# A SwiGLU down product in fp32: eight block products of 512 columns become seven of 256 columns

## The chip, the core and the metric

The kernel runs on one core of one Trainium2 chip. The metric is the device time of one execution in microseconds. Before the change it is 600.21 us (median of three runs, 599.43 to 602.72). A core has five engines with queues of their own: PE (TensorE, matmuls; its weight loads are shown apart as PEld), DVE (VectorE), ACT (ScalarE), POOL (GpSimd) and SP, which here issues all the DMAs. Matmuls read SBUF and write PSUM, of which the feed-forward part uses eight tiles of 512 fp32 columns by 128 partitions (called banks below). All of POOL's operations in this kernel are on SBUF.

## The reference, cut to what matters

```python
x = A_q                                   # 2048 tokens x 512
h = _layernorm(x) * (1 + ca) + sa
x = x + ga * _A_ref(h, ...)               # a long causal convolution: first 200 us of the kernel
h = _layernorm(x) * (1 + cb) + sb
g = _silu(h @ w_gate)                     # 512 x 1792
u = h @ w_up
x = x + gb * ((g * u) @ w_down)           # 1792 x 512
```

Everything is fp32. The change concerns the last three lines, the feed-forward network, for the second half of the tokens.

## The kernel before, in words

**Precision.** A matmul here takes operands in the format fp32r. Each operand x is kept as two tensors, a high part (x copied to fp32r by ACT) and a low part (x minus the high part, by DVE or POOL). A product is three passes: low by high, high by low, high by high (`PASSES`, line 633). `wd_hi` and `wd_lo` (lines 620, 624) do it for a piece of w_down, `finish` (line 707) for an activation.

**Tiling.** The 1792 hidden columns are 14 blocks f of 128; two blocks are a group g (G = 2, seven groups). The 2048 tokens are two halves q of 1024, each of them two tiles t of 512 (xt[0] to xt[3], in which the result is accumulated). The program writes out n = 2 to 27, with q = n // 14 and f = n % 14 (loop at line 1415): first all blocks of the first 1024 tokens, then all of the second.

**Gate and up.** For one block, `gate_up` (line 714) computes gate and up for both token tiles at once by a 2x2 block scheme of seven products in place of eight. `seventh` (line 637) is one of them: six matmuls of 512 columns into one PSUM bank. The products run in the order 1, 5, 7, 2, 3, 6, 4 in the banks a, b, c, a, b, d, c; DVE adds them up, ACT applies silu, DVE multiplies gate by up. The weights' operands (three blocks A and four sums S, high and low) are made by `split_w` (line 585): casts on ACT, sums and low parts on POOL. It is done anew for each token half.

**Down.** `down` (line 648) is one 128-token block i of one tile t: six matmuls of 512 columns (two blocks f, three passes) into one bank, then a DVE addition to xt. Eight such downs make a group, 48 matmuls. They are put between the products of the two blocks after the group's end (`downs`: one behind product 7, one behind product 3, two behind product 6). The last group's eight come at the very end, and each then stores its rows.

**Order.** Each engine runs its instructions in the order in which the program writes them (`keep_in_program_order`), and each waits only for its data and buffers. What is not part of a block's own chain is hung behind one of its products: `at[k]` is a list of calls made behind product k. In n, `split_w(n + 1)` and `load_w(n + 2)` hang behind product 7, and behind product 3 comes the split of w_down for a group (odd f) or its load (even f). Loads go through SP in program order.

Of the kernel before, what the change touches and what calls it, by code (L numbers as in the profile page):

```python
# [10 lines left out]
F32 = mybir.dt.float32  # L11
F32R = mybir.dt.float32r
AF = mybir.ActivationFunctionType
ALU = mybir.AluOpType
# [41 lines left out]
def adaln_h3_swiglu(ctx, tc, q, kT, vT, shk, ssm, dskip, wgu, wdn, c, wmod, e_fwd, e_inv, w_c, out):  # L56
# [12 lines left out]
    homes8 = iter(  # L69
        "401235670135260172635162432634623634642623634642652376243652376243"  # L70
    )

    def e8(shape, dt, name):
        return wp.tile(shape, dt, tag=f"e8_{next(homes8)}", name=name, bufs=1)

    def r4(shape, dt, name):
        return wp.tile(shape, dt, tag="r4", name=name, bufs=5)
# [31 lines left out]
    def one(name):  # L109
        return ffn["p"].tile([P, 512], F32, tag="one", name=name) if "p" in ffn else bank(name)  # L110
# [474 lines left out]
    def split_w(f):  # L585
# [11 lines left out]
        s = e8([P, 2, 4, 2, P], F32R, "wsum")  # L597
# [6 lines left out]
        o = AOP[f] = {n: w[:, :, i] for i, n in enumerate(("A11", "A12", "A22"))}  # L604
        o.update({n: s[:, :, i] for i, n in enumerate(("S1", "S2", "S3", "S4"))})

    def w8_hi(f):

# [11 lines left out]
    def wd_hi(g):  # L620
        wt = WD[g] = e8([P, 2, G, D], F32R, "wd")
# [6 lines left out]
    def split_wd(g):  # L628
        wd_mul(g)
        wd_hi(g)  # L630
        wd_lo(g)

    PASSES = ((1, 0), (0, 1), (0, 0))
    PROD = {1: ("A11", "B11"), 2: ("A12", "B21"), 3: ("S4", "B22"), 4: ("A22", "T4"),
# [32 lines left out]
    def downs(n):  # L667
        for _ in range(min(n, len(todo))):
            down(*todo.pop(0))

    GU, SG = {}, {}

# [34 lines left out]
    def finish():  # L707

        if late:
            h, c_ = late.pop()  # L710
            act.copy(h[:, 0], c_)
            dve.tensor_tensor(h[:, 1], c_, h[:, 0].bitcast(F32), op=ALU.subtract)

    def gate_up(q, f, at={}):


        def behind(n):
            for fn in at.get(n, ()):
                fn()

        a = one("a")
        seventh(a, f, 1)
        p1 = g2("p1")
        act.copy(p1, a)
        behind(1)
        b = one("b")
        seventh(b, f, 5)
        p5 = g2("p5")
        act.copy(p5, b)
        finish()  # L730
        behind(5)
        c_ = one("c")
        seventh(c_, f, 7)
        dve.tensor_tensor(p5, p5, c_, op=ALU.add)
        behind(7)
        downs(1)
        seventh(a, f, 2, True)
        sg1 = g2("sg1")
        act.activation(sg1, a, AF.Silu)
        behind(2)  # L740
        seventh(b, f, 3, True)
        behind(3)
        downs(1)
        d = one("d")
        seventh(d, f, 6)
        dve.tensor_tensor(p1, p1, d, op=ALU.add)
        sg2 = g2("sg2")
# [4 lines left out]
        downs(2)  # L752
        dve.tensor_tensor(d, sg2, d, op=ALU.mult)
        h2 = acts[q, f, 1] = slots.pop(0)
        act.copy(h2[:, 0], d)
        seventh(c_, f, 4, True)
        dve.tensor_tensor(h2[:, 1], d, h2[:, 0].bitcast(F32), op=ALU.subtract)
        dve.tensor_tensor(c_, p1, c_, op=ALU.add)
        dve.tensor_tensor(c_, sg1, c_, op=ALU.mult)
        h1 = acts[q, f, 0] = slots.pop(0)  # L760
        late.append((h1, c_))
        behind(4)


    csil = cp.tile([P, 4], F32, name="csil")
    csb = cp.tile([P, 4, 32], F32, name="csb")

    def load_shk():
        sp.dma_start(shk_sb, shk.rearrange("(b p) t -> p b t", p=P))
# [30 lines left out]
        t = SS[c_][0:1, 0, :]  # L800
        dve.tensor_tensor(t, t, dsk[:, c_ * P : (c_ + 1) * P], op=ALU.add)

    wc = cp.tile([P, 384], F32, name="wc")
    WX, WK = wc[:, 0:96], wc[:, 96:192]
    def load_wc():
        sp.dma_start(wc, w_c)
# [573 lines left out]
    def release(n):  # L1380
# [31 lines left out]
        (14, 7): lambda: diff("B21", "B21", "B11"),  # L1412
        (14, 2): lambda: then("T4", "B21"),
    }
    for n in range(G, 2 * NF):
        q, f = n // NF, n % NF

        at = {k: [AT[n, k]] if (n, k) in AT else [] for k in range(1, 8)}
        if n + 1 < 2 * NF:
            at[7].append(lambda nf=(n + 1) % NF: split_w(nf))  # L1420
            if n + 2 < 2 * NF:
                at[7].append(lambda nf=(n + 2) % NF: load_w(nf))
            if f % G == G - 1:
                at[3].append(lambda g=(n + 1) % NF // G: split_wd(g))
            elif n + 2 < 2 * NF:
                at[3].append(lambda g=((n + 2) % NF) // G: load_wd(g))
        gate_up(q, f, at)
        if f % G == G - 1:
            todo += [(q, f // G, t, i) for t in (1, 0) for i in range(4)]
    finish()  # L1430
    downs(8)

# [55 lines left out]
```

## Time and profile before

| | |
|---|---|
| median of three runs | 600.21 us (599.43 to 602.72) |
| profiled execution, span | 598.0 us (first to last instruction; the execution's own time outside the span is not in the profile) |
| instructions | 10148 |
| granted PE clock, mean | 0.992 |
| DVE, ACT, POOL busy | 457.0, 302.7, 329.9 us |
| DMA | 69.00 MB in all |
| second half of the tokens | from about 388 us on |

PE's busy time counts modelled ends of matmuls; the starts are measured, so how often one starts is a better measure of its cost. In the timeline, "x6" is a run of six instructions merged into one line, with the start of the first and the time until the end of the last, and a bracket tells how long the engine stood idle before it and who ended that. In the groups, the number after the bar is the busy time in us, then the mean of one in ns. In the table of stretches a line has the stretch, its length, then for PE, PEld, DVE, ACT and POOL the busy us with the number of instructions, the granted clock of PE, the DMA share and GB/s.

### The profile page before, as it was taken

Reading aid. Unit: us, or ns where it says so; the run is one execution under the profiler, and the core shown is the slowest. Engines: PE = TensorE matmul, PEld = TensorE weight load, DVE = VectorE, ACT = ScalarE, POOL = GpSimd, SP = SyncE. Lnnn points to the kernel's source line nnn. Section 1 sums busy time; section 2 is a strip of 40 time slices with the busy share of each in tenths; the row PEclk is TensorE's granted clock in tenths of the full one; section 3 lists DMA queues with packets and bytes.
Section 4 is the critical chain, followed back from the end, with each engine's and each line's share of the span. In section 5 each row is a group of like instructions: output and inputs, shape, how many; then the busy total and the mean of one; then the engine's idle time right before and its main releaser. Section 6 shows DMA issues by size and latency. Waiting matters only on the chain.

```text
span 598.0 us, 10148 instructions
## 1 busy us (share of the span) xinstructions
PE 583.2 (98%) x4132; PEld 455.0 (76%) x4132; DVE 457.0 (76%) x585; ACT 302.7 (51%) x443; POOL 329.9 (55%) x264
## 2 busy tenths in 40 slices
PE   5999999999999999999999999999999999999997
PEld 4955756535988888888888888788888888888875
DVE  6999989978968878787778868975656565656555
ACT  1897989953574454445544435443434343434320
POOL 0003269692395896757467765766747474747200
PEclk7999999999999999999999999999999999999999
DMA  8998999999011021212120201243212110210003
GB/s 289 412 392 308 227 340 299 210 332 172 33 41 65 21 92 35 71 36 71 36 71 35 71 36 36 71 144 103 71 36 70 36 70 37 70 36 0 1 1 140
DMA packets 35423, 69.00 MB, mean 115 GB/s; under 512 B 2481, under 2 KB 18993, under 8 KB 33074
## 3 DMA queue, kind: packets, MB, share of 16 engines
q1 hardware_dynamic: 35378, 68.37, 37.0%
q8 instruction: 32, 0.52, 0.4%
q14 instruction: 13, 0.11, 0.1%
HBM read 55.78 MB, written 12.58 MB: 114 GB/s over the span
## 4 chain that ended last, share of the span: by engine, by line
PE 85%; DMA 6%; ACT 3%; DVE 2%; SPq 2%; issue 2%; ACTq 0%; DVEq 0%
PE dn L40 25%; PE a L40 12%; PE b L40 11%; PE c L40 11%; PE d L40 6%; PE s L40 5%; PE g L40 3%; DMA X<-away 2%; PE iv L40 2%; PE y L40 2%; PE px L40 2%; PE pk L40 2%; SPq L40 2%; DMA away<-X 2%; PE kt L40 1%
## 5 line engine op out<-in xcount | busy, mean ns | idle before, releaser
L40 PE MATMUL dn<-wd,acts 128*128 128x512 f32 x672 | 166.4, 391 | 0.5 <-DVE acts L40 0.4
L40 PEld LDWEIGHTS dn<-wd,acts 128*128 128x128 f32 x672 | 125.7, 188 | 27.6 <-DVE acts L40 1.1
L40 POOL TENSOR_TENSOR wa<-ws,wa 128x512 fp32r<-128x512 f32 (+1 forms) x52 | 61.7, 1209 | 111.8 <-ACT wa L40 104.0
L40 DVE TENSOR_TENSOR x<-x,dn 128x512 f32<-128x512 f32 x112 | 74.9, 681 | 50.6 <-PE dn L40 49.4
L40 PE MATMUL b<-op,wsum 128*128 128x512 f32 x312 | 79.2, 389 | 0.0
L40 POOL TENSOR_TENSOR wsum<-sr,wsum 128x1024 fp32r<-128x1024 f32 x26 | 71.4, 2745 | 0.0
L40 PEld LDWEIGHTS b<-op,wsum 128*128 128x128 f32 x312 | 58.5, 188 | 12.2
L40 ACT ACTIVATE sg<-sg 128x512 f32<-128x512 f32 x26 | 16.5, 633 | 85.4 <-DVE sg L40 85.4
L40 PE MATMUL a<-op,wa 128*128 128x512 f32 x228 | 57.9, 389 | 0.0
L40 PEld LDWEIGHTS a<-op,wa 128*128 128x128 f32 x228 | 42.8, 188 | 8.9
L40 DVE STREAM_TRANSPOSE X<-X 128x1024 f32<-128x1024 f32 x20 | 46.2, 2338 | 1.1 <-ACT X L40 1.1
L40 ACT CAST acts<-d 128x512 fp32r<-128x512 f32 x26 | 15.3, 587 | 62.5 <-DVE d L40 38.1
L40 POOL TENSOR_TENSOR vt<-u,vt 128x512 f32<-128x512 f32 x8 | 10.1, 1303 | 64.9 <-DMA x<-in_q 50.8
L40 POOL TENSOR_TENSOR s<-s,bcs 128x1024 f32<-128x1024 f32 x16 | 38.8, 2449 | 9.5 <-ACT s L40 9.3
L40 POOL TENSOR_TENSOR sr<-ws 128x256 f32<-128x256 f32 x52 | 43.5, 837 | 0.0
L40 POOL TENSOR_TENSOR wd<-wds,wd 128x1024 fp32r<-128x1024 f32 x14 | 35.4, 2529 | 9.6 <-ACT wd L40 9.6
L40 PE MATMUL c<-op,wa 128*128 128x512 f32 x156 | 39.7, 390 | 0.0
L40 PE MATMUL d<-op,wsum 128*128 128x512 f32 x156 | 39.6, 389 | 0.0
L40 PE MATMUL c<-op,wsum 128*128 128x512 f32 x156 | 39.6, 389 | 0.0
L40 DVE TENSOR_TENSOR acts<-c,acts 128x512 fp32r<-128x512 f32 x26 | 18.0, 692 | 21.5 <-ACT acts L40 21.5
L40 PEld LDWEIGHTS c<-op,wa 128*128 128x128 f32 x156 | 29.2, 188 | 6.3 <-DVE op L40 0.3
L40 PEld LDWEIGHTS d<-op,wsum 128*128 128x128 f32 x156 | 29.3, 188 | 6.1
(109 smaller groups left out, 1089.0 us busy)
## 6 DMA issues: line engine op xcount, KB each, us to landing
ws<-in_wgu SPq DMA_DIRECT2D x28, 512.0 KB, 3.2
wds<-in_wdn SPq DMA_DIRECT2D x14, 512.0 KB, 3.3
wm<-in_wmod SPq DMA_DIRECT2D x6, 1024.0 KB, 13.7
away<-X SPq DMA_DIRECT2D x3, 2048.0 KB, 10.4
X<-away SPq DMA_DIRECT2D x12, 512.0 KB, 11.2
x<-in_q SPq DMA_DIRECT2D x4, 1024.0 KB, 12.8
out<-x SPq DMA_DIRECT2D x16, 256.0 KB, 2.1
kt<-in_kT SPq DMA_DIRECT2D x3, 1024.0 KB, 7.1
```

Of the source, the lines that this page charges most:

```text
L40: return lambda *a, **k: self.tc.keep_in_program_order(f(*a, **k))
```

## The change

For groups 0 to 5 of the second 1024 tokens the down product is done by seven block products too. The two token tiles are the rows of blocks, the two blocks f of the group the inner index (L11 = the activation of tile 0 for the first f, L12 for the second f, L21 and L22 for tile 1), and w_down's group is cut into R11, R12, R21, R22, whose columns are the halves of 256 of the 512 output columns. S1 to S4 are sums of L's, T1 to T4 sums of R's:

```python
DOWN = {1: ("L11", "R11"), 2: ("L12", "R21"), 3: ("S4", "R22"), 4: ("L22", "T4"),
        5: ("S1", "T1"), 6: ("S2", "T2"), 7: ("S3", "T3")}
HALVES = {"y": (1, 7), "z": (5, 6), "x0": (2, 3), "x1": (4,)}
```

`part_down` does one or two of these products for 128 tokens: three matmuls of 256 columns each, side by side in one bank. Parts x0 and x1 are added to xt[2] and xt[3] by DVE; y and z, which are needed in several places of the result, are accumulated over the six groups in two SBUF tiles (ACT copies for group 0, DVE additions afterwards):

```diff
+    def part_down(g, i, to):
+        o = one("dq")
+        ns = HALVES[to]
+        for h, n in enumerate(ns):
+            a, b = LOP[g][DOWN[n][0]], ROP[g][DOWN[n][1]]
+            for k, (xa, wa) in enumerate(PASSES):
+                pe.matmul(
+                    o[:, h * H : h * H + H], a[:, xa, i * P : (i + 1) * P], b[:, wa],
+                    start=(h == k == 0), stop=(k == 2), skip_group_check=True,
+                )
...
+    PARTS = ({"c1": 3, "a2": 2, "b2": 2, "d": 3, "c2": 2}, {"a1": 4})
```

PARTS says where the 16 parts of a group go: twelve into the next block with even f (three behind product 7, two behind 2, two behind 3, three behind 6, two behind 4), in the order y, z, x1, x0, and the four x0 parts behind product 1 of the block with odd f.

The activations of these groups stay raw in SBUF, and their sums and high and low parts are made behind the blocks. `hi_lo` is an ACT cast and a subtraction on the engine named:

```diff
+    def first_of(f, t, raw):
+        o = LOP.setdefault(f // G, {})
+        if t:
+            RAW["L21"] = raw
+            return
...
+        dve.tensor_tensor(s3, raw, RAW["L21"], op=ALU.subtract)
+        o["L11"] = slots.pop(0)
+        hi_lo(o["L11"], raw, pool)
+    def second_of(f, t, raw):
+        o = LOP[f // G]
+        if t:
+            s1, s2 = RAW["L21"], RAW["S3"]
+            dve.tensor_tensor(s1, s1, raw, op=ALU.add)
+            dve.tensor_tensor(s2, raw, s2, op=ALU.subtract)
+            for n, r, e in (("S1", s1, dve), ("S2", s2, dve), ("L22", raw, pool)):
+                o[n] = slots.pop(0)
+                hi_lo(o[n], r, e)
+            return
+        s4 = RAW.pop("L21")
+        dve.tensor_tensor(s4, raw, RAW.pop("S3"), op=ALU.subtract)
+        for n, r, e in (("S4", s4, pool), ("L12", raw, dve)):
+            o[n] = slots.pop(0)
+            hi_lo(o[n], r, e)
```

S3's parts are made by `third_sum` (ACT and POOL). In `gate_up`, the sum p5 + p1 and the product of gate and up are now written to SBUF for these groups, where they went to PSUM:

```diff
-        dve.tensor_tensor(d, p5, p1, op=ALU.add)
+        dve.tensor_tensor(p5 if ops else d, p5, p1, op=ALU.add)
...
+        if ops:
+            dve.tensor_tensor(sg2, sg2, p5, op=ALU.mult)
+            done(f, 1, sg2)
+            seventh(c_, f, 4, True)
+            dve.tensor_tensor(c_, p1, c_, op=ALU.add)
+            dve.tensor_tensor(sg1, sg1, c_, op=ALU.mult)
+            late.append((lambda raw: done(f, 0, raw), sg1))
```

w_down of these groups is prepared by `sum_wd` (POOL: scaling of 1024 elements per partition and four sums of 256) and `pairs_wd` (ACT: three casts; POOL: low parts of 256, 1024 and 512).

The operands of gate and up are no longer made twice. In the first half, block f's are also stored to DRAM by `keep_w` (two DMAs, 768 and 1024 KB, behind product 2); in the second, blocks 2 to 13 get them back by `fetch_w` (behind product 1 of the block before) and no `split_w` is done for them.

The last group is done as before, but its w_down is loaded and split in its own two blocks (before: a group earlier), and y and z are brought into the result there by four folds, each one operation of 4x256 elements per partition on POOL and one on DVE:

```diff
+    def fold(k):
...
+        if k == 0:
+            pool.tensor_tensor(zb, zb, ya, op=ALU.add)
+            dve.tensor_tensor(x0a, x0a, ya, op=ALU.add)
+        elif k == 1:
+            pool.tensor_tensor(yb, yb, zb, op=ALU.add)
+            dve.tensor_tensor(x0b, x0b, za, op=ALU.add)
+        elif k == 2:
+            pool.tensor_tensor(x0b, x0b, zb, op=ALU.add)
+            dve.tensor_tensor(x1b, x1b, za, op=ALU.add)
+        else:
+            pool.tensor_tensor(x1a, x1a, yb, op=ALU.add)
+            dve.tensor_tensor(x1b, x1b, yb, op=ALU.add)
...
+            else:
+                at[7].append(lambda: split_wd(g1, 4))
+                at[2].append(lambda: fold(0))
+                at[3].append(lambda: fold(1))
+                at[6].append(lambda: fold(2))
+                at[4].append(lambda: fold(3))
```

Downs of the first half keep their places; the homes of some SBUF tiles change, and two small tiles (`csb`, `wc`) move to a pool that is freed before the feed-forward network.

More of the change, by code (lines that the diff above doesn't have):

```diff
@@ L583, in load_wd, with keep_w, operands, fetch_w @@
         stage["d", g] = st
-    def split_w(f):
+    kept = {}
+    def keep_w(f):
+        w, s = WS[f]
+        kept[f] = []
+        for t in (w, s):
+            m = dp.tile([P, t.shape[1], t.shape[2], t.shape[3], P], F32, tag=f"kept{f}_{len(kept[f])}", name="kept")
+            sp.dma_start(m, t.bitcast(F32))
+            kept[f].append(m)
+    def operands(f, w, s):
+        o = AOP[f] = {n: w[:, :, i] for i, n in enumerate(("A11", "A12", "A22"))}
+        o.update({n: s[:, :, i] for i, n in enumerate(("S1", "S2", "S3", "S4"))})
+    def fetch_w(f, home):
+        w = ffn["s"].tile([P, 2, 3, 2, P], F32R, tag="wa", name="wa", bufs=2)
+        s = e8([P, 2, 4, 2, P], F32R, "wsum", home)
+        for t, m in zip((w, s), kept.pop(f)):
+            sp.dma_start(t.bitcast(F32), m)
+        operands(f, w, s)
+    WS = {}
+    def split_w(f, home=None):
         st = stage.pop(f)
@@ L710, in finish, with gate_up @@
             h, c_ = late.pop()
-            act.copy(h[:, 0], c_)
-            dve.tensor_tensor(h[:, 1], c_, h[:, 0].bitcast(F32), op=ALU.subtract)
-    def gate_up(q, f, at={}):
+            if callable(h):
+                h(c_)
+            else:
+                acts[h] = slots.pop(0)
+                h = acts[h]
+                act.copy(h[:, 0], c_)
+                dve.tensor_tensor(h[:, 1], c_, h[:, 0].bitcast(F32), op=ALU.subtract)
+    def gate_up(q, f, at, fill):
         def behind(n):
@@ L719, in behind @@
                 fn()
+        ops = q == 1 and f // G < NG - 1
+        done = first_of if f % G == 0 else second_of
         a = one("a")
@@ L735, in gate_up @@
         behind(7)
-        downs(1)
+        fill("c1")
         seventh(a, f, 2, True)
@@ L1428, in adaln_h3_swiglu, with fill @@
+        if m == 1:
+            acts2 = b16("acts2", (P, 4, 2, 512), F32R)
+            slots.extend(acts2[:, k] for k in range(4))
+        def fill(where):
+            if m < G:
+                downs(WHOLE.get(where, 0))
+            else:
+                part_downs(PARTS[m % G].get(where, 0))
+        gate_up(q, f, at, fill)
         if f % G == G - 1:
-            todo += [(q, f // G, t, i) for t in (1, 0) for i in range(4)]
+            if q and f // G < NG - 1:
+                todo2 += [(f // G, i, to) for to in ("y", "z", "x1", "x0") for i in range(TB)]
+            else:
+                todo += [(q, f // G, t, i) for t in (1, 0) for i in range(4)]
```

142 lines of the change are left out of this document (110 added, 32 removed).

## The prediction

> **What bounds the kernel now.** I read the page's head first, then the busy time by stretches, then the timeline of one block of the FFN, then its last 18 us.
>
> ```profile
> span 598.0 us, 10148 instructions
> PE 583.2 (98%) x4132; PEld 455.0 (76%) x4132; DVE 457.0 (76%) x585; ACT 302.7 (51%) x443; POOL 329.9 (55%) x264
> ```
>
> ```profile
> 400.00:500.00 100.00, 100.00 (x442) 82.81 (x442) 62.54 (x91) 39.87 (x66) 63.01 (x53) 1.00 0.19 64
> 500.00:570.00 70.00, 70.00 (x310) 57.99 (x309) 44.00 (x64) 25.12 (x42) 37.09 (x31) 1.00 0.08 30
> 570.00:598.00 28.00, 23.50 (x101) 18.53 (x100) 14.44 (x22) 3.28 (x6) 0.00 (x0) 0.96 0.20 75
> ```
>
> The columns are length, then busy us of PE, PEld, DVE, ACT and POOL, the granted clock, the DMA share and GB/s. From 400 to 570 us, where the second 1024 tokens are worked on, PE is busy all the time at full clock, while DVE has 63 of 100 us. So matmuls that go away here are time won, as long as nobody else becomes late. How long a matmul really takes is read from starts, since the ends are modelled:
>
> ```profile
> 433.61 1.52 PE L40 MATMUL b<-op,wsum 128*128 128x512 f32 x6
> ...
> 448.57 1.52 PE L40 MATMUL b<-op,wsum 128*128 128x512 f32 x6
> ```
>
> The same product comes back after 14.96 us, and a block has 42 matmuls of gate and up and four downs of six: 14.96/66 = 0.2267 us for one of 512 columns.
>
> **Matmuls: down by 4.8 us.** One group's down product takes 48 matmuls of 512 columns, 48 x 0.2267 = 10.88 us. The change makes it 7 products x 4 token blocks x 3 passes = 84 matmuls of 256 columns, each with a weight load of its own. No matmul of 256 columns in this format is in the trace. The nearest rows are short matmuls that also load 128x128 weights each time:
>
> ```profile
> 60.73 2.09 PE L40 MATMUL kvt<-ident,vt 128*128 128x128 f32 x16
> 62.65 1.06 PE L40 MATMUL kt<-ident,kt 128*128 128x128 f32 x8
> 63.54 1.02 PE L40 MATMUL pb<-part,sel 128*128 128x512 f32 x2
> ```
> ```profile
> 62.53 0.98 PEld L40 LDWEIGHTS kt<-ident,kt 128*128 128x128 f32 x8
> ```
>
> Start to start, kvt takes 1.92/16 = 0.120 us and kt 0.89/8 = 0.111 us, loads included. That is the least that load and matmul together have shown: 84 x 0.111 = 9.32 us, a gain of 1.56 a group. From the other side, half of 0.2267 is 0.113, if all of it belongs to the columns; every ns of it that belongs to the matmul itself adds half a ns. 33 ns of that kind would make 0.130 and the gain nothing (10.92 us). I take 0.120, between these and also the kvt row: 84 x 0.120 = 10.08, so 0.80 a group and **-4.8 us** for six; the ends are -9.3 and +0.2.
>
> The Trainium skill's page TensorE: Matmul & The Clock Gate, section Back-to-back issue gap, gives 262 cycles for 256 columns, 109 ns at 2.4 GHz, and the sum would be -10.3 us by it; its 518 cycles for 512 columns, 216 ns, are less than the 0.2267 us of this trace.
>
> **DVE and POOL in the six groups: hidden, by little.** Durations are from the groups in one pair of blocks (408.4 to 438.4 us):
>
> ```profile
> L40 DVE TENSOR_TENSOR x<-x,dn 128x512 f32<-128x512 f32 x9 | 6.1, 685 | 6.5 <-PE dn L40 6.4
> L40 DVE TENSOR_TENSOR d<-p,p 128x512 f32<-128x512 f32 x2 | 1.8, 921 | 0.0
> L40 POOL TENSOR_TENSOR sr<-ws 128x256 f32<-128x256 f32 x4 | 3.0, 740 | 0.0
> L40 POOL TENSOR_TENSOR wd<-wds,wd 128x1024 fp32r<-128x1024 f32 x1 | 2.4, 2411 | 0.0
> L40 ACT CAST wd<-wds 128x1024 fp32r<-128x1024 f32 x1 | 1.0, 1049 | 0.1
> L40 ACT CAST acts<-d 128x512 fp32r<-128x512 f32 x2 | 1.2, 588 | 4.2 <-DVE d L40 2.2 <-PE c L40 2.0
> ```
> ```profile
> 421.87 2.00 POOL L40 TENSOR_TENSOR wa<-ws,wa 128x512 fp32r<-128x512 f32 x2 [7.71 <-ACT wa L40]
> ```
>
> DVE has, per pair of blocks, 26 operations of 512 (18 in gate and up, 8 additions) and one scaling. Afterwards it has 14 in gate and up, 7 that make S1 to S4 and low halves, 12 additions of 512 and 4 of 256: 33 x 0.685 + 4 x 0.42 (estimate: 0.685 less 256 elements at the slope between 512 and 1024) = 24.3 us. PE needs 84 x 0.2267 + 10.08 = 29.1 us for the pair. POOL loses the weight splits and gets two operations of 1024, five of 512 (2.00 - 0.74 = 1.26) and five of 256: 4.8 + 6.3 + 3.7 = 14.8 us. ACT stays near half. On busy time PE still ends last. But DVE and POOL hinder each other:
>
> ```profile
> 365.08 2.39 POOL L40 TENSOR_TENSOR wsum<-sr,wsum 128x1024 fp32r<-128x1024 f32 x1
> ...
> 365.15 3.40 DVE L40 TENSOR_TENSOR op<-hraw,op 128x1024 fp32r<-128x1024 f32 x1 [1.29 <-ACT op L40]
> ...
> 368.48 1.22 DVE L40 TENSOR_TENSOR wds<-wds,bcs 128x1024 f32<-128x1024 f32 x1
> ```
> ```profile
> 444.05 0.69 DVE L40 TENSOR_TENSOR sg<-p,b 128x512 f32<-128x512 f32 x1
> 444.65 0.69 DVE L40 TENSOR_TENSOR d<-p,p 128x512 f32<-128x512 f32 x1
> ```
>
> Undisturbed, a DVE operation of 1024 with both inputs in SBUF takes 1.22 us. The one at 365.15 takes 3.40: POOL's runs until 367.47, and it ends 1.08 later. So the two exclude each other, one whole instruction at a time. With one input in PSUM (x<-x,dn) DVE does not wait. Operations of the first kind go from 3 to 11 per pair (p5+p1, gate times up, the S sums, three low halves). At the mean surplus of d<-p,p here, 0.23 us, that is 2.5 us more for DVE, 26.8, under 29.1: nothing on PE. As independent operations follow each other by 0.60 (444.05, 444.65), 24.3 is high by some. Two covers carry this. The additions may lag behind the parts by up to five of the eight PSUM tiles (the products hold three). And POOL has to finish L11, three halves of R and T, and S3 (1.26 + 0.74 + 2.41 + 1.26 + 1.26 = 6.9 us) between product 5 of the odd block, at 5.6 us, and the first y part of the next, at 16.5. If they fail, PE waits; a rival.
>
> **Stored weights: nothing.** keep_w writes 768 + 1024 KB per block in the first half, fetch_w reads them in the second.
>
> ```profile
> wds<-in_wdn SPq DMA_DIRECT2D x14, 512.0 KB, 3.3
> ...
> away<-X SPq DMA_DIRECT2D x3, 2048.0 KB, 10.4
> X<-away SPq DMA_DIRECT2D x12, 512.0 KB, 11.2
> ```
>
> By the rows of away 1792 KB take 9.1 us of a 14.96 us block; as a read (four issues are one 2048 KB tile) 9.8 us of the shorter, 12.4 us block that follows its buffers' release. On SP the store stands between load_w and load_wd; what it reads was made a block earlier, so it holds them up only for two issues. If a fetch came late, PE would wait at the next block's first product. On POOL sum_wd waits for a load of the same block (3.3 us to landing); behind it stands L11's low half, which is not due before the y parts of the block after the next.
>
> **The end: up by 8.8 us.** In the last block, load and split of the last w_down (before: a group earlier) and four folds of y and z are new, on DVE and POOL, and no downs lie behind product 6 any more.
>
> ```profile
> 580.49 1.52 PE L40 MATMUL c<-op,wa 128*128 128x512 f32 x6
> ...
> 581.85 1.36 PE L40 MATMUL dn<-wd,acts 128*128 128x512 f32 x4
> ...
> 583.43 10.31 PE L40 MATMUL dn<-wd,acts 128*128 128x512 f32 x44 [0.22 <-DVE acts L40]
> ```
>
> Now PE reaches the eight closing downs at 581.85 and, 4 matmuls in, waits for the low half of the last activation: 583.43 - 581.85 - 4 x 0.2267 = 0.67 us lost. Afterwards, with zero at the last block's start: products and four x0 parts (2.88) put product 7's end at 6.96 and PE's arrival at the downs at 12.4. On DVE the low half of the block before and p5 += c (0.69 each) are done at 8.3, the scaling (1.22) at 9.5, fold 0 (1.22) at 10.7. Then DVE still has fold 1, p5+p1 and fold 2 of the SBUF kind (1.2 + 0.6 + 1.2 = 3.0) in front of gate times up, while POOL's queue holds the low half of w_down and four folds of 2.4 each. If POOL gets two turns in between, DVE is free at 10.7 + 3.0 + 4.8 = 18.5, and gate times up, ACT's cast and the low half (0.69 + 0.59 + 0.69) end near 20.5. Three or four matmuls run before; 44 x 0.2267 = 9.97 end at 30.5, against 12.4 + 10.88 + 0.67 = 23.95 now: **+6.5 us**. With three turns it is +8.9, with none (p1 += d and the sum sg2, 1.4, then show) the low half ends near 17.0: +3.1. I take two, since the folds of POOL are 2.4 and DVE has three places where it can lose. PE also stands still long enough for its clock:
>
> ```profile
> 5.00:8.60 3.60, 0.13 (x1) 0.00 (x0) 2.58 (x3) 0.20 (x1) 0.00 (x0) 1.00 1.02 378
> 8.60:15.40 6.80, 4.51 (x39) 4.30 (x41) 6.66 (x8) 1.45 (x3) 0.00 (x0) 0.50 1.05 388
> ```
> ```profile
> 10.88 5.28 PE L40 MATMUL s<-er,ss 64*128 64x128 f32 x48 [5.76 <-DMA er<-in_e_fwd]
> ```
>
> A gap of 5.76 us brought a clock of 0.50 until 15.4, that is 4.5 us of work at half speed, 2.3 lost. The gap at the end is about as long (13.3 to 19.8): **+2.3 us**, between 0 and 3.4.
>
> **Sum**: -4.8 + 6.5 + 2.3 = +4.0 us on a span of 598.0. The median of the runs is 600.2, 2.2 us above the profiled span (launch and the spread of runs, 599.4 to 602.7), so 604.2 us. A measurement of this kernel can tell about 0.5% from no change, 3.0 us: the band is 597.2 to 603.2.
>
> **Rivals.**
> Cheap short matmuls and a mild end (the other side): parts follow each other by 0.111 as kt does, and at the end POOL's turns fall where DVE does other work. -9.3 + 3.1, no clock loss: 594.0. For it: the kt row, and DVE's two operations on PSUM between the folds. Against: POOL's four folds in a row. It decides from a closing gap under about 5 us. Chance 0.18.
> Cheap short matmuls with the end as forecast: -9.3 + 8.8 = -0.5, 599.7; 0.18. My 0.120 with the mild end: -4.8 + 3.1, 598.5; 0.05.
> DVE and POOL late in each group: the mean of d<-p,p over the whole run is
>
> ```profile
> L40 DVE TENSOR_TENSOR d<-p,p 128x512 f32<-128x512 f32 x26 | 30.8, 1184 | 0.0
> ```
>
> a surplus of 0.49, and with it 24.3 + 11 x 0.49 = 29.7 us against 29.1, plus PE's waits where POOL's S3 is late; 0.8 a group with these is +4.8, 609.0. For it: 84% of DVE's time is spoken for, in an order fixed by hand. 0.12.
> The smaller matmul is not cheaper per column (0.130): +0.2 + 8.8, 609.2; the change then saves no PE time at all, 0.02.
> Weight loads as the bound: a load shows 188 ns,
>
> ```profile
> L40 PEld LDWEIGHTS dn<-wd,acts 128*128 128x128 f32 x48 | 9.0, 188 | 1.9
> ```
>
> and 84 x 0.188 = 15.8 us a group, +29.5 + 8.8, 638.5. Against: kt's eight loads fit in 0.98 us. 0.03. The Trainium skill's page Perfetto Trace Analysis, section Identifying the Most-Contended Engine, judges TensorE by the busy share of these loads, which would count against this change; the kt rows show loads that overlap.
>
> **Numbers.** The forecast has the remaining 0.42. Slower by over 0.5%: 0.12 + 0.02 + 0.03 and most of the forecast's 0.42 (0.35, since it lies 1.0 us from the band's edge): 0.52. Within: 0.18 + 0.05 + 0.07 = 0.30. Faster: 0.18. The range is 594 to 613 us: from the fast rival to the late groups with 0.130 (604.2 + 5.0 + 4.8 = 614.0, nearly); the forecast's own is 600 to 608.
>
> **What would show it.** Part matmuls 0.120 apart; pairs of blocks near 29.1 us instead of 29.92; DVE over 80% busy there with two-SBUF operations stretched past 1 us; a PE gap of 6 to 8 us in front of the last 44 downs, with POOL's folds and DVE's in turns inside it, and a granted clock of 0.5 behind it. I am wrong in the main if the closing gap is under 3 us, or if PE waits in front of y or z parts in every group.

## The result, and the profile after

The changed kernel takes 606.19 us (median of six runs, 603.29 to 608.41) against 600.77 us of six runs of the kernel before on the same chip (599.43 to 602.72). The ratio is 1.0084, with a 95% interval of 1.0054 to 1.0113: slower, by 0.8%. The profiled execution took 604.08 us and its span is 602.3 us, 4.3 us more than before.

The page's head, and the busy time by stretches (columns as before; the last row is a stretch inside the third):

```profile
span 602.3 us, 10735 instructions
PE 583.9 (97%) x4348; PEld 465.6 (77%) x4348; DVE 492.5 (82%) x641; ACT 299.2 (50%) x445; POOL 324.4 (54%) x250
```
```profile
400.00:500.00 100.00, 99.89 (x573) 87.87 (x572) 74.99 (x115) 39.44 (x70) 48.86 (x39) 1.00 0.42 155
500.00:570.00 70.00, 69.62 (x406) 61.22 (x405) 57.92 (x93) 22.11 (x39) 28.99 (x24) 1.00 0.32 121
570.00:602.30 32.30, 22.88 (x84) 17.42 (x84) 24.23 (x29) 4.43 (x7) 14.89 (x5) 0.88 0.17 65
584.05:590.90 6.85, 5.98 (x13) 4.43 (x14) 5.13 (x6) 1.17 (x2) 6.85 (x3) 0.50 0.00 0
```

In the six groups (the first two rows) PE is still busy nearly all the time, but no longer all of it: 0.11 us are missing in the first 100 us and 0.38 in the next 70. DVE went from 62.5 to 75.0 us of 100, POOL from 63.0 to 48.9, and the DMA share from 0.19 to 0.42. In the last 32 us PE works only 22.9, and 6.8 us of that stretch have a granted clock of 0.50.

To compare kernels, the span is cut at starts of matmuls that all of them have. "n = 2 to 12" is the time between the starts of product 6 of these two blocks, and so on; "groups" runs from the start of product 6 of block n = 14 to the start of the last block's product 4, "end" from there to the start of the last matmul, "tail" from there to the end of the span. (Block n = 14, the first of the second half, begins at 371.6 us in before; the 388 us given further up are near the start of n = 15.) What stands in front of block n = 2 (about 202 to 208 us) differs between executions of kernels that are alike there, by up to 5 us, so single spans can't be compared to better than that; the stages can. In us:

| kernel | n = 2 to 12 | n = 12 to 14 | groups | end | tail |
|---|---|---|---|---|---|
| before | 148.02 | 30.64 | 198.70 | 12.87 | 4.63 |
| after | 148.06 | 29.92 | 196.62 | 20.91 | 4.34 |

The change gains 2.1 us in the six groups and 0.7 at the border of the two halves, and loses 8.0 at the end.

**The short matmuls**, from the timeline of the second group's y parts (three matmuls a row):

```profile
434.14 0.52 PE L40 MATMUL dq<-wda,acts 128*128 128x256 f32 x3
...
434.50 0.52 PE L40 MATMUL dq<-wdt,acts 128*128 128x256 f32 x3
```

Three starts take 0.36 us, so one matmul of 256 columns takes 0.120 us.

**The wait in the groups**, 4 us later in the same timeline:

```profile
438.33 1.29 POOL L40 TENSOR_TENSOR acts<-l,acts 128x512 fp32r<-128x512 f32 x1 [1.61 <-ACT acts L40]
...
438.81 1.36 DVE L40 TENSOR_TENSOR acts<-sg,acts 128x512 fp32r<-128x512 f32 x1 [1.21 <-ACT acts L40]
...
440.50 1.90 PE L40 MATMUL dq<-wdt,acts 128*128 128x256 f32 x12
440.69 2.47 DVE L40 TENSOR_TENSOR y<-y,dq 128x512 f32<-128x512 f32 x4
441.42 0.77 PEld L40 LDWEIGHTS dq<-wdt,acts 128*128 128x128 f32 x6 [0.25 <-DVE y L40]
```

DVE comes to the first y addition only at 440.69, although the first y part (the six matmuls from 434.14 on) was computed before 435.2. Right before it stands the low half of L12: DVE stood idle for 1.21 us until ACT had made its high half, and then waited for POOL's low half of S4 (1.36 us instead of 0.69). By then the parts hold all the banks that the products leave, and the weight load at 441.42 shows the 0.25 us that PE stands still. The same wait shows in the groups after it, five times in all; in the first group ACT copies y and z to SBUF, and PE does not wait. A pair of blocks takes 29.55 us, 0.37 less than the 29.92 before.

**The end**, around product 4 of the last block (577.04):

```profile
576.36 1.22 DVE L40 TENSOR_TENSOR x<-x,z 128x1024 f32<-128x1024 f32 x1
576.53 3.27 POOL L40 TENSOR_TENSOR wd<-wds,wd 128x1024 fp32r<-128x1024 f32 x1 [18.70 <-ACT wd L40]
...
577.04 1.52 PE L40 MATMUL c<-op,wa 128*128 128x512 f32 x6
...
578.81 1.55 DVE L40 TENSOR_TENSOR d<-p,p 128x512 f32<-128x512 f32 x1
...
579.76 2.79 POOL L40 TENSOR_TENSOR z<-z,y 128x1024 f32<-128x1024 f32 x1
...
579.86 0.96 PE L40 MATMUL dn<-wd,acts 128*128 128x512 f32 x3 [1.29 <-POOL wd L40]
580.27 3.37 DVE L40 TENSOR_TENSOR x<-x,z 128x1024 f32<-128x1024 f32 x1
...
583.56 0.68 DVE L40 TENSOR_TENSOR d<-sg,d 128x512 f32<-128x512 f32 x1
584.28 0.59 ACT L40 CAST acts<-d 128x512 fp32r<-128x512 f32 x1 [4.66 <-DVE d L40]
...
584.92 13.42 PE L40 MATMUL dn<-wd,acts 128*128 128x512 f32 x45 [4.10 <-ACT acts L40]
```

PE waits three times: 1.29 us for the low half of w_down, 4.10 for ACT's cast of the last activation, and 0.44 more (in its weight loads) for the low half. Behind the cast stands DVE's chain: its addition p5+p1 (578.81) waits for POOL's low half of w_down, its third fold (580.27) for POOL's first, and only then comes gate times up (583.56). The 45 matmuls then take 13.42 us, where 44 took 10.31 before.

**The transfers** of the stored weights, by the list of DMA issues (KB each, median us to landing):

```profile
kept<-wsum SPq DMA_DIRECT2D x12, 1024.0 KB, 6.4
wsum<-kept SPq DMA_DIRECT2D x12, 1024.0 KB, 6.4
kept<-wa SPq DMA_DIRECT2D x12, 768.0 KB, 5.6
wa<-kept SPq DMA_DIRECT2D x12, 768.0 KB, 4.3
```

No wait of PE in the groups has a DMA as its releaser.

### The profile page after: what moved, and what is told of

Read it like the earlier page. It is cut to its first block, busy times and chain, and to the rows that moved or that the text cites. A ratio compares the mean times of both kernels' runs of the same rounds, so it can differ in the third digit from the quotient of the medians.

```text
span 602.3 us, 10735 instructions
## 1 busy us (share of the span) xinstructions
PE 583.9 (97%) x4348; PEld 465.6 (77%) x4348; DVE 492.5 (82%) x641; ACT 299.2 (50%) x445; POOL 324.4 (54%) x250
## 4 chain that ended last, share of the span: by engine, by line
PE 76%; DVE 12%; DMA 5%; ACT 3%; issue 2%; SPq 1%; DVEq 0%; ACTq 0%
PE dn L40 15%; PE b L40 9%; PE a L40 9%; PE c L40 9%; PE dq L40 6%; PE d L40 5%; PE s L40 4%; DVE p L40 3%; PE g L40 3%; PE px L40 3%; PE iv L40 3%; PE pk L40 3%; PE y L40 2%; DVE acts L40 2%; DMA X<-away 2%; DVE sg L40 2%
## 5 line engine op out<-in xcount | busy, mean ns | idle before, releaser
L40 PE MATMUL dn<-wd,acts 128*128 128x512 f32 x384 | 97.5, 399 | 5.4 <-ACT acts L40 4.1
L40 PEld LDWEIGHTS dn<-wd,acts 128*128 128x128 f32 x384 | 73.5, 193 | 21.9 <-ACT acts L40 4.5
L40 POOL TENSOR_TENSOR wa<-ws,wa 128x512 fp32r<-128x512 f32 (+1 forms) x28 | 36.7, 1330 | 48.8 <-ACT wa L40 48.8
L40 DVE TENSOR_TENSOR x<-x,dn 128x512 f32<-128x512 f32 x64 | 42.3, 679 | 16.4 <-PE dn L40 16.2
L40 POOL TENSOR_TENSOR acts<-sg,acts 128x512 fp32r<-128x512 f32 x12 | 15.6, 1297 | 71.3 <-ACT acts L40 71.3
L40 PE MATMUL dq<-wdt,acts 128*128 128x256 f32 x288 | 42.6, 284 | 0.3
L40 PEld LDWEIGHTS dq<-wdt,acts 128*128 128x128 f32 x288 | 38.9, 191 | 2.8 <-DVE y L40 1.3
L40 DVE TENSOR_TENSOR p<-p,d 128x512 f32<-128x512 f32 x26 | 17.7, 682 | 27.5 <-PE d L40 27.5
L40 POOL TENSOR_TENSOR wsum<-sr,wsum 128x1024 fp32r<-128x1024 f32 x14 | 37.6, 2688 | 0.0
L40 PEld LDWEIGHTS c<-op,wsum 128*128 128x128 f32 x156 | 29.3, 188 | 6.1
```

The costliest lines, as they stand in the source:

```text
L40: return lambda *a, **k: self.tc.keep_in_program_order(f(*a, **k))
```

## The experiments

The theory was the prediction's: the seven products win a little in every group, and the four folds and the late w_down at the end lose more, half of it by DVE and POOL excluding each other and a part by the clock. The rivals: the stored weights cost something, the folds are innocent, the clock is innocent.

### No folds

It leaves out the folds, so what y and z hold is missing in the result.

```diff
-                at[2].append(lambda: fold(0))
-                at[3].append(lambda: fold(1))
-                at[6].append(lambda: fold(2))
-                at[4].append(lambda: fold(3))
```

> The changed kernel without its four folds, on DVE and on POOL (y and z are not brought into the result). Theory (the closing gap comes from the folds, which DVE must pass in front of the last block's gate times up, and for which it waits in turns with POOL): PE's waits in front of the closing downs shrink from 5.8 us to about 2, the clock stays full, and the time falls by 4 to 6 us against the changed kernel, to just under the kernel before. Rival (the bare chain after product 6, silu, multiplication, cast and subtraction, with no downs left to cover it, and the late split of w_down): the gap stays over 4 us and the time falls by under 1.5 us.

Measured: 600.38 us, ratio to before 1.0009 (0.998 to 1.0038); groups 196.56, end 14.52, tail 4.27. The closing matmuls in its timeline:

```profile
584.03 0.98 PE L40 MATMUL dn<-wd,acts 128*128 128x512 f32 x3 [0.42 <-POOL wd L40]
...
586.00 0.49 PE L40 MATMUL dn<-wd,acts 128*128 128x512 f32 x1 [1.00 <-ACT acts L40]
...
586.73 10.27 PE L40 MATMUL dn<-wd,acts 128*128 128x512 f32 x44 [0.23 <-DVE acts L40]
```

The waits shrink to 0.42, 1.00 and 0.23 us, the clock stays at 1.00 there and 44 matmuls take 10.27 us. The folds are 6.4 of the 8.0 us of the end, and the time falls by 5.8 us against after, as the theory said. The other 1.6 go with the late low half of w_down and with the two downs that no longer lie behind product 6; no run parts these two.

### POOL's folds earlier

```diff
+                for k in (0, 1, 3):
+                    at[1].append(lambda k=k: fold(k, "pool"))
+                at[5].append(lambda: fold(2, "pool"))
...
-                at[2].append(lambda: fold(0))
...
+                at[2].append(lambda: fold(0, "dve"))
...
```

DVE's four stay where they were.

> POOL's four fold operations move ahead of the split of w_down, to products 1 and 5 of the last block, where POOL stands idle; DVE's four stay where they are and are as many. Theory (DVE and POOL exclude each other, so DVE loses POOL's turns): the closing gap shrinks by 2.8 to 3.5 us, and the time by 3 to 5 us with the clock's part. Rival (DVE's own time for its folds is the price): the gap stays within 0.5 us.

Measured: 605.86 us, ratio 1.0103 (1.006 to 1.0147); end 18.91. In the timeline of the last block:

```profile
574.54 2.39 POOL L40 TENSOR_TENSOR x<-x,z 128x1024 f32<-128x1024 f32 x1
...
575.48 2.54 DVE L40 TENSOR_TENSOR wds<-wds,bcs 128x1024 f32<-128x1024 f32 x1
...
582.55 1.65 PE L40 MATMUL dn<-wd,acts 128*128 128x512 f32 x3 [2.62 <-POOL wd L40]
```

Neither number came out: the end is 2.0 us shorter than in after, where the theory had 2.8 to 3.5 and the rival at most 0.5, and the medians (605.86 and 606.19) can't tell the two kernels apart. POOL's last fold now meets DVE's scaling of w_down, which takes 2.54 us instead of 1.22, and the chain behind it, w_down's low half included, is late by 1.3. The collision moved from one DVE operation to another; the clock fell to 0.50 here as well. So this run doesn't tell what POOL's turns alone cost.

### Matmuls that fill the gap

```diff
     finish()
+    warm(50)
     downs(8)
```

These are 100 short matmuls in the trace.

> 50 dummy matmuls of 128 columns (about 5.5 us) in front of the closing downs, in the time that PE waits there. Theory (the wait halves PE's clock for the downs behind it): the granted clock stays at 1, the closing 44 downs' matmuls take 10 us in place of 12.3 and the time falls by about 2 us though nothing else has changed. Rival (no clock loss that matters): the time stays or rises by up to 1 us.

Measured: 607.24 us, ratio 1.0125 (1.0098 to 1.0152); end 23.20. In the timeline:

```profile
579.68 11.33 PE L40 MATMUL warm<-ident 128*128 128x128 f32 x100
590.76 11.14 PE L40 MATMUL dn<-wd,acts 128*128 128x512 f32 x48
```

They were too many: 11.33 us in a gap of some 6, so the time rose instead of falling by 2 us. But the clock stays at 1.00, and all 48 closing matmuls take 11.14 us where 45 took 13.42. With fewer of them:

```diff
     finish()
+    warm(20)
     downs(8)
```

> The kernel after with 40 short matmuls on the identity (4.4 us by the 0.1105 us that one took in the run with 100) in front of the closing downs; nothing else differs. Theory: of the end's loss 2 to 2.6 us are the clock that falls to 0.50 behind the gap. With the dummies over before the activation comes, PE waits a second or two, the clock stays 1.00, the closing 45 matmuls take 10.5 to 11.2 us instead of 13.42, 18.3 to 18.7 us from the start of the last product 4 to the last matmul instead of 20.9, and 603.8 us. Rival: the slow closing matmuls are a wait on DVE and POOL that the lower clock only goes with: they take over 13 us again, 606 us.

Measured: 603.53 us, ratio 1.0046 (1.0019 to 1.0072); end 18.52, 2.39 us less than in after. In the timeline:

```profile
581.06 4.63 PE L40 MATMUL warm<-ident 128*128 128x128 f32 x40
...
587.59 0.51 PE L40 MATMUL dn<-wd,acts 128*128 128x512 f32 x1 [1.21 <-ACT acts L40]
...
588.32 10.29 PE L40 MATMUL dn<-wd,acts 128*128 128x512 f32 x44 [0.22 <-DVE acts L40]
```

The activation is as late as before, yet the 44 matmuls behind it take 10.29 us, as in the kernel before. So the lower clock cost 2.4 us by itself, and dummy work wins exactly that.

### The stored weights alone

The kernel before, with its downs of eight, plus `keep_w` and `fetch_w` in place of the second half's `split_w`.

```diff
+        if n < NF:
+            at[2].append(lambda f=f: keep_w(f))
+        if n + 1 < NF + 2:
+            at[7].append(lambda nf=(n + 1) % NF: split_w(nf))
+        elif n + 1 < 2 * NF:
+            at[1].append(lambda nf=(n + 1) % NF: fetch_w(nf))
...
-            at[7].append(lambda nf=(n + 1) % NF: split_w(nf))
...
```

> The kernel before with the stored weights alone: gate and up operands are written to memory in the first half and fetched in the second, the down product stays as it was. Theory (the transfers are hidden and POOL's and ACT's relief moves nothing, since PE sets the pace): within 1.5 us of the kernel before. Rival (the stored weights by themselves bring or cost time): over 2 us either way.

Measured: 599.95 us, ratio 0.9985 (0.9961 to 1.001); stages 148.09, 30.69, 198.73, 12.83 and 3.99, as before (the tail by 0.6). Storing and fetching 12 x 1792 KB costs nothing and wins nothing by itself. It also shows that the 0.7 us at the border (30.69 here, 29.92 in after) don't come from the stored weights.

### The seven products without stored weights

```diff
-        if n < NF:
-            at[2].append(lambda f=f: keep_w(f))
...
-            at[1].append(lambda nf=m + 1: fetch_w(nf, 2 if nf % 2 else 6))
-        if n + 2 < NF + 2:
+            at[7].append(lambda nf=m + 1: split_w(nf, 2 if nf % 2 else 6))
+        if n + 2 < 2 * NF:
```

> The kernel after without stored weights: gate and up weights are split anew for the second half, as before did, and the seven down products are as in after. Theory: POOL gets two splits of 7.4 us per pair of blocks on top of 15.1 us, 29.9 us of a pair's 29.55, so it has no slack and w_down's parts or S3's low half come late in each group: a pair takes 31 us or more, 9 us or more over six groups, 615 us or more. So the stored weights are what makes room for the seven products. Rival: POOL's work fits because PE's waits are not on its path every time and its 30 us spread over the pair: 606 to 609 us, and the stored weights do nothing.

Measured: 668.53 us, ratio 1.1144 (1.1095 to 1.1193); groups 260.18, 63.6 us more than in after; a pair takes some 40.7 us. The sign was right, the size far beyond the 31 us a pair that the theory gave as the least. The three largest of PE's waits in the second half (us in total, times, longest), and a stretch of 30 us with the columns of the table of stretches:

```profile
PE dq L40 <- ACT sg L40: 10.9, 5, 2.2
PE dq L40 <- POOL acts L40: 9.3, 6, 3.0
PE b L40 <- POOL wsum L40: 9.0, 5, 1.8
```
```profile
430.00:460.00 30.00, 23.49 (x113) 18.73 (x111) 17.01 (x24) 12.40 (x22) 22.39 (x20) 0.94 0.12 36
```

POOL is busy 22.4 of 30 us. The theory had it full; it is not. PE waits for POOL, ACT and DVE in turn, and which of these queues sets the pace no run shows. The mean granted clock is 0.94, so there are stretches of 0.50 too. The stored weights win nothing alone, but the seven products can't be had without them in this order.

### DVE's folds late as well

```diff
-                at[2].append(lambda: fold(0))
-                at[3].append(lambda: fold(1))
-                at[6].append(lambda: fold(2))
-                at[4].append(lambda: fold(3))
+                for k in (3, 2, 0, 1):
+                    at[4].append(lambda k=k: fold(k, "dve"))
```

POOL's folds are placed as in the second experiment.

> POOL's folds stand behind products 1 and 5 of the last block, DVE's four folds behind product 4, after gate times up of both halves and in front of the low half of the last activation. Theory: what made the closing gap are DVE's three folds in front of gate times up and the waits for POOL among them. Then gate times up comes about as early as without folds: PE waits 1.5 to 2.5 us in front of the closing matmuls instead of 5.8, no stretch at clock 0.5, 14.5 to 15.5 us from the start of the last product 4 to the last matmul instead of 20.9, and 600 to 601 us where after had 606.2. Rival: DVE and POOL take turns on what both read and write in SBUF whatever the order, 4 x 2.4 + 4 x 1.2 = 14.4 us for the folds, so the wait only moves, now to the low half of the last activation, which stands behind 4.9 us of folds: a second PE gap of 2 us or more among the closing matmuls, 17 us or more, 603 us.

Measured: 600.72 us, ratio 1.0021 (0.9992 to 1.0051); end 16.95. In the timeline:

```profile
573.35 2.39 POOL L40 TENSOR_TENSOR x<-x,z 128x1024 f32<-128x1024 f32 x1
...
574.27 2.55 DVE L40 TENSOR_TENSOR wds<-wds,bcs 128x1024 f32<-128x1024 f32 x1
...
589.71 4.83 PE L40 MATMUL dn<-wd,acts 128*128 128x512 f32 x20 [0.82 <-DVE acts L40]
```

Both were right in part. The first gap falls from 5.8 to 2.9 us (1.69 for w_down's low half, which the collision at 574.27 still delays, 0.99 for the cast, 0.23 for the low half) and the clock stays at 1.00. But four folds now stand in front of the last low half, and PE waits 0.82 us for it. The end of 16.95 us is near the rival's 17, the time is the theory's.

### L12's low half on POOL

```diff
-        for n, r, e in (("S4", s4, pool), ("L12", raw, dve)):
+        for n, r, e in (("S4", s4, pool), ("L12", raw, pool)):
```

> The kernel after with one operation moved: the low half of L12 is made by POOL, where DVE made it right in front of the first y addition. Theory: the 0.25 to 0.3 us that PE waits for DVE in each group's y and z parts come from there (DVE stood idle 1.21 us for ACT's cast and then 0.67 us behind POOL), so they go: a pair of blocks takes 29.2 us instead of 29.55, 2 us less over six groups, about 604.2 us. Rival 1: the wait comes from DVE's load as a whole, and the next late operation takes its place: no difference, 606.2. Rival 2: on POOL's queue the 1.3 us delay the scaling and sums of w_down, and x0 or T parts come late: PE waits in front of x0 parts, 607 or more.

Measured: 602.19 us, ratio 1.0039 (1.0019 to 1.006); groups 194.48, end 20.90. A pair takes 29.24 us. The place in the timeline that answers to the one of after:

```profile
438.32 2.48 DVE L40 TENSOR_TENSOR y<-y,dq 128x512 f32<-128x512 f32 x4
...
440.69 1.60 PE L40 MATMUL dq<-wdt,acts 128*128 128x256 f32 x12
```

The y additions start some 2.4 us earlier, and twelve short matmuls take 1.60 us instead of 1.90. The groups win 2.14 us more with one word changed, as the theory said. (By the medians it is 4 us, but they come from two series; the stages say 2.1.)

### A new order at the end

The scaling of the last w_down goes to POOL and into the block before, its cast into a buffer that is free earlier; POOL's folds stand behind products 1 and 5 and DVE's behind the last low half. `last_downs` does four closing downs at once, for the first f, then for the second:

```diff
+                else:
+                    at[6].append(lambda: wd_mul(g1, pool))
...
-                at[7].append(lambda: split_wd(g1, 4))
-                at[2].append(lambda: fold(0))
...
+                at[1].append(lambda: wd_hi(g1, 5))
+                at[1].append(lambda: fold(0, "pool"))
+                at[1].append(lambda: fold(1, "pool"))
+                at[1].append(lambda: wd_lo(g1))
+                at[5].append(lambda: fold(2, "pool"))
+                at[5].append(lambda: fold(3, "pool"))
...
-    downs(8)
+    for t in (1, 0):
+        for k in (3, 2) if t else (0, 1):
+            fold(k, "dve")
+        last_downs(t)
```

> The kernel after with a new order at the end alone: the last w_down is scaled by POOL behind product 6 of the block before (DVE did it behind product 7 of the last), cast behind product 1 into a buffer that is free earlier, POOL's folds lie between product 1 and 5 of the last block with the low half of w_down among them, DVE's folds stand behind the last activation's low half, and the closing matmuls do the first of the two blocks f for four downs before the second. Theory: the end's loss is one of order only, each wait has a place where it costs nothing. PE then waits under 0.8 us at the end, 12.3 to 13.2 us from the start of the last product 4 to the last matmul (before: 12.9, after: 20.9), no stretch at clock 0.5, and 597.5 to 599 us. Rival: POOL has 2.4 x 6 = 14.4 us of work between the z parts' end and the closing matmuls (about 13 us), it ends late and w_down's low half or DVE's addition p5+p1 waits for it: a PE gap of 2 to 4 us, 600.5 to 602.5 us.

Measured: 600.05 us, ratio 1.0002 (0.9977 to 1.0026); groups 196.70, end 12.31, tail 7.79. PE does its 48 closing matmuls in 11.34 us in one row, with one wait of 0.42 us in its weight loads, and the end is shorter than before the change, as the theory had it. But the tail is 3.4 us longer than in after, which the theory had not counted, and its 597.5 to 599 us were missed. With L12's low half on POOL as well:

> The edits of the two kernels before it together (L12's low half on POOL, and the new order at the end). Theory: they are independent, so the gains add up: 606.2 - 2 - 8 = 596.2 us, 0.7% under before (600.8), of which the six groups give 4 us, the place of the first half's last w_down 0.7, and the end nothing or a little. Rival: POOL, with 1.3 us more per pair and 14.4 us at the end, falls behind in the last pair: then it is no better than the new order alone, 598 to 599 us.

Measured: 598.52 us, ratio 0.9963 (0.994 to 0.9986); groups 194.48, end 12.31, tail 7.77. The gains of the stages add up, but the theory's 596.2 us were missed by 2.3, since the longer tail stays. The 598 to 599 us of the rival came out for another reason than its own: POOL did not fall behind (the groups and the end are as short as in the runs with one edit). The last rows of its timeline:

```profile
585.65 1.98 PE L40 MATMUL dn<-wd,acts 128*128 128x512 f32 x8
...
588.07 1.22 DVE L40 TENSOR_TENSOR x<-x,z 128x1024 f32<-128x1024 f32 x1
589.39 2.48 DVE L40 TENSOR_TENSOR x<-x,dn 128x512 f32<-128x512 f32 x4
```

The last matmul ends at 587.63 (a modelled end), but DVE still has a fold and all four additions of tile 0 to do: these four downs end close together, and the folds came first.

### The version that beats both

Tile 0's downs one after the other again, one fold of DVE given to POOL a block earlier, one put between two of POOL's, one into DVE's wait for the last cast:

```diff
+                    at[6].append(lambda: fold(4, "pool"))
...
+                at[3].append(lambda: fold(2, "dve"))
...
+                at[4].append(lambda: fold(1, "dve"))
...
+    fold(3, "dve")
+    last_downs(1)
+    del todo[:4]
+    downs(4)
```

> The kernel with both edits (L12's low half on POOL, new order at the end), changed where its tail was long: there the four downs of tile 0 also did the first f of all four before the second, so all ended together, and DVE had 10.4 us of folds and additions after the last low half. Here tile 0's downs go one after the other again, one DVE fold goes to POOL (behind product 6 of the block before the last), one between POOL's last two folds, one into DVE's wait for the last cast. Theory: the 3.4 us by which its tail was longer than in after (7.77 against 4.34) were that: the tail is 4.0 to 4.6 us again, 12.3 to 12.6 us from the start of the last product 4 to the last matmul, and 595 us, 0.9% under before. Rival: DVE's fold between POOL's two moves POOL's last one into DVE's addition p5+p1, and gate times up comes 1 to 2 us later: PE waits 1 to 2 us among the closing matmuls and the time is 596 to 597 us.

Measured: 594.82 us (593.7 to 597.64) against 600.91 of before, ratio 0.9908 (0.988 to 0.9937); groups 194.56, end 12.37, tail 4.80. The tail is 3.0 us shorter, if a little over the 4.0 to 4.6 us expected. In the timeline:

```profile
571.81 2.44 DVE L40 TENSOR_TENSOR x<-x,z 128x1024 f32<-128x1024 f32 x1
...
573.11 3.40 POOL L40 TENSOR_TENSOR x<-x,y 128x1024 f32<-128x1024 f32 x1
...
576.10 11.40 PE L40 MATMUL dn<-wd,acts 128*128 128x512 f32 x48
576.26 0.80 DVE L40 TENSOR_TENSOR d<-p,p 128x512 f32<-128x512 f32 x1
```

DVE's fold takes its turn between two of POOL's, at a time when DVE has nothing else to do, and POOL's last one ends at 576.51, so that p5+p1 loses 0.1 us. The same eight additions that cost 6.4 us in after cost nothing seen on PE here. The change as it was made is slower, and its idea, put in order, is 0.9% faster.

## Why the prediction was right, and where it was not

The forecast of 604.2 us and slower was right, and so were the two mechanisms on which its sign rested: a small gain by short matmuls, and a larger loss at the end by DVE, POOL and the clock. The sum for the span was +4.0 us. The two profiled spans differ by 4.3, all stages from n = 2 on by 5.0, and the medians by 5.4. That closeness is partly luck: the six groups won 2.7 us less than forecast, an unforeseen 0.7 was won at the border, the end lost 0.8 less, and the tail came out 0.3 shorter.

**Matmuls (-4.8).** The price of 0.120 us came out to the last digit, but as a choice between 0.111 and 0.130, which is partly luck: kt and kvt, the rows that it leaned on, are transposes against the identity in the kernel (`pe.transpose`), not products. What failed is the step behind it, "DVE and POOL in the six groups: hidden, by little". The busy sums in it were good (24.3 us for DVE and 14.8 for POOL per pair; 23.90 and 15.14 were measured between 437.95 and 467.50). But a sum of busy time under PE's says nothing of the order. DVE had an operation that waits for ACT right in front of the y additions, and POOL's turn on top of that. The text did count five spare banks as a cover; DVE's first y addition came 5.5 us behind the first part, and that used them up. This cost 29.55 - 29.24 = 0.31 us in each of five groups, and 0.6 us once behind the last x0 parts, where PE waited for DVE again (0.29 us in the row at 570.07); both went when the one operation was moved. The remaining 0.12 a pair to the forecast 29.12 is left without an experiment; a product that follows parts takes 1.38 us instead of 1.36 in the starts, and there are six such per pair. "PE waits in front of y or z parts in every group" was named as what would prove the forecast wrong in the main; it happened in five of the six, at two fifths of the 0.8 us per group at which it was a rival. The time came out near the forecast all the same, since the end weighs more.

**DVE and POOL by turns.** Right, and seen in single rows: the same operation of 1024 elements on DVE took 1.22 us at 576.36 and 3.37 at 580.27, with POOL's fold running until 582.55. In the groups it is p5+p1 that pays:

```profile
430.20 1.31 POOL L40 TENSOR_TENSOR acts<-s,acts 128x512 fp32r<-128x512 f32 x1
430.23 1.82 DVE L40 TENSOR_TENSOR p<-p,p 128x512 f32<-128x512 f32 x1
```

1.82 us instead of 0.68, and it doesn't show on PE, as forecast. The Trainium skill, page SBUF — State Buffer, section Who interferes with whom, says that a DVE instruction with two SBUF inputs contends with a GpSimd instruction that reads SBUF, that what they share is an exclusive lock, and that issue order decides who blocks. The rows here agree: POOL's starts first, and DVE's ends 0.54 us after POOL's end at 431.51, where it takes 0.68 alone.

**Stored weights (nothing).** Right: ratio 0.9985 with them alone. What the text did not say is that they are the condition of the rest: without them 668.5 us.

**The end (+8.8).** 8.0 were measured. The step was worked out from the last block's start: low half of the activation ready 20.5 us later. It was ready at 585.59, 20.2 us after that start (565.36), with two turns of POOL in between as taken. They cost 3.0 us (1.55 - 0.68 at 578.81 and 3.37 - 1.22 at 580.27) instead of 4.8, as DVE came to each when POOL's operation was already under way. The 1.8 us saved there were nearly made up by two things that the sum had not: p1 += d and the sum sg2, left out where POOL gets two turns (1.3 us, 577.49 to 578.81), and fold 0, done 0.4 us later than forecast. So the agreement of 20.2 with 20.5 is partly luck too. PE's wait of 1.29 us for w_down's low half was not foreseen; it lies inside the same gap, and by this reading costs nothing of its own, since the cast comes later. The folds' 6.4 us (by the kernel without them) contain the clock's 2.4 (by the dummies; forecast 2.3).

**Not foreseen:** 0.7 us at the border of the halves. There the kernel before, and the one with the stored weights alone (30.69 us), prepare a w_down for the second half in n = 12 and 13, which after does later. In the trace of before, p5+p1 of n = 13 (371.52) takes 2.36 us behind POOL's low half of this w_down, gate times up comes late, and so does the activation of the first downs of n = 14:

```profile
375.00 0.68 DVE L40 TENSOR_TENSOR d<-sg,d 128x512 f32<-128x512 f32 x1
...
375.63 1.28 PE L40 MATMUL dn<-wd,acts 128*128 128x512 f32 x4
...
377.13 0.73 PE L40 MATMUL dn<-wd,acts 128*128 128x512 f32 x2 [0.23 <-DVE acts L40]
```

Four starts of 0.2267 us end at 376.54; the fifth matmul starts 0.59 us later, and in after these six follow each other without a wait. That is a reading of traces; no run moves this w_down alone.

## What to carry to other kernels

Busy sums tell whether an engine can keep up, not whether it does: look in its queue at what stands right in front of the operation that sets a buffer free, and move from there whatever waits for a third engine. Work without a due time (the folds) belongs where its engine is idle and the engine that it excludes is, too; the same eight operations cost 6.4 us in one order and nothing that shows on PE in another. And when the last stretch is mended, look at the tail behind it: work taken off PE's path can end up behind PE's last matmul.

## What the runs showed of the hardware

The two matmul prices, 0.2267 us for 512 columns and 0.120 for 256, give a line of 0.417 ns per column and 13 ns per matmul, each with a weight load. Two prices fix a line and don't test it; the dummies of 128 columns, 0.111 us apart in the run with 100, are no third point, as their operand `ident` is plain fp32 and each call shows as two matmuls. The Trainium skill, page TensorE: Matmul & The Clock Gate, section Back-to-back issue gap, has the same slope (N/2.4 ns) but 2.5 ns as the fixed part; by its 216 and 109 ns, an estimate, a group would save 1.2 us (48 x 0.216 - 84 x 0.109) where the trace's prices give 0.8.

The clock fell to 0.50 for 6.83 us at the end of after, 3.2 us into PE's wait of 4.10. In the second experiment it fell 2.1 us into a wait of 2.62. Waits of 1.69, 0.99 and 0.23 us close together did not bring it, nor 4.63 us of dummy matmuls followed by 1.21 us of waiting. Where the limit lies between these was not tried. In the clock's records of the trace the stretches between two changes are multiples of 3.41 us (566.61, 6.83 and 10.24 in after): the clock changes by that step. It does not come back with the work: in after the matmuls went on at 584.92 and the clock rose at 590.88.

In the places seen here, DVE waiting for POOL's turn got the next one though POOL had more queued: in the last version, from 571.81 to 576.51, DVE's fold went between two folds of POOL (POOL's second shows 3.40 us, 1.0 of it waiting), and in after DVE's fold of 580.27 went between POOL's of 579.76 and 582.63.
